# A gated attention block on one core: the up products of two token tiles made together, as seven block products instead of eight

## The chip, the cores and the metric

The kernel runs on one core of a Trainium2 chip. The metric is the time of one execution on the device, in microseconds (us); the lower, the better. A core has TensorE (PE in the profile; its weight loads are PEld), VectorE (DVE), ScalarE (ACT), GpSimd (POOL) and SyncE (SP, which issues most of the DMAs). Each engine works off its own queue in order.

## What is computed

Both branches see the same normalised tokens. One is attention over the last 512 rows of a cache with 32 heads, the other an MLP with a squared relu, which gates the first.

```python
xn = _layernorm(x, axis=-1)                    # x: 2048 tokens x 640
s = _A_ref(xn, A_k_cache, A_v_cache, A_wq, A_wo)   # attention, 32 heads of 128, times wo
h = jnp.einsum("bsd,df->bsf", xn, w1) + b1     # 640 -> 1728
r = jnp.where(h > zero, h, zero)
h = r * r
out = jnp.einsum("bsf,fd->bsd", h, w2) + b2    # 1728 -> 640
return x + s * _silu(out)
```

## The kernel before

Everything lies transposed: features on the 128 partitions, tokens along a row. The 2048 tokens are four tiles of 512 (`NT`). D = 640 is five slices of 128 (`DC`), and F = 1728 is fourteen chunks (`FC`): thirteen of 128, and one of 64 that stands fourth in the order (`rp`, line 66).

TensorE multiplies in a shortened form of float32 (`F32R`). To keep the precision, each operand is split in two: a high part, which ACT makes by a copy into that form, and a low part, the difference, which VectorE or GpSimd makes with two inputs from SBUF. A product is then three matmuls (high by high, high by low, low by high: `triple`, line 560, and `products`, line 97) of 128 x 128 by 128 x 512. The chunk of 64 packs both parts of the weights side by side and needs two.

The work has two stages.

1. **MLP of the first three tiles** (`mlp_step`, line 483, over `steps`, line 464). A step (t, f) makes one chunk of the hidden layer, `up` (line 416): 15 matmuls into a bank `ph`; ACT adds the bias and the relu, GpSimd squares, ACT and VectorE split the square (`square_split`, line 383). It then makes `down` (line 448) of the step before, 15 matmuls into five banks `py` that collect over all chunks. So the split of h has the time of one down and one up. All of w1 and w2 is split during the first tile (`split_w`, line 373) and stays in SBUF. The normalisation of the next tile runs beside (`ln_load`, `ln_block`, `ln_var`, `ln_root`, `ln_rows`, `ln_chunk`, lines 141 to 202), and each tile's split input is stored for attention (`spill`, line 338). After its last chunk a tile's gate is made (`gate`, line 467) and stored.
2. **Attention** (from line 538), 128 units of one head and one tile, laid out by a plan with hand-set times, with parts of the fourth tile's MLP before and behind it.

The order is set in two ways. Instructions given through `Ordered` (line 69: `pe`, `dve`, `act`, `pool`, `sp`) keep the order in which they are written, on their engine. Those given through `nc.tensor`, `nc.vector` and so on may be moved by the scheduler when the program is built, within what their data allow. `pe.addr_align` puts the next instruction of TensorE at a chosen place in a block of 256 instructions, with empty ones ahead of it; attention relies on it (`align`, line 1035), and `LEAD_STEPS` (line 22) spreads empty ones over some steps ahead.

PSUM has eight banks of 128 x 512: two for `ph`, five for `py`, one (`psx`) for odd jobs.

Of the kernel before, what the change touches and what calls it, by code (L numbers as in the profile page):

```python
# [21 lines left out]
LEAD_SLOT, LEAD_PADS, LEAD_STEPS = 76, 5, range(19, 23)  # L22
# [3 lines left out]
def kernel(  # L26
# [24 lines left out]
    LN_AT = {t: (3, 7) if t == LATE else (5, 9) for t in range(1, NTILE)}  # L51
# [45 lines left out]
    def products(ps, pairs, first=True, last=True):  # L97
        n = len(pairs)
        for i, ((ah, al), (bh, bl)) in enumerate(pairs):
            nc.tensor.matmul(ps, ah, bh, start=first and i == 0, stop=False)  # L100
            nc.tensor.matmul(ps, ah, bl, start=False, stop=False)  # L101
            nc.tensor.matmul(ps, al, bh, start=False, stop=last and i == n - 1)  # L102

    psx = ctx.enter_context(tc.tile_pool(name="psx", bufs=1, space=PSUM))

    FO, FA = FC - 3, FC - 4
    keep = ctx.enter_context(tc.tile_pool(name="keep", bufs=1))
    mctx, wctx, hctx = ExitStack(), ExitStack(), ExitStack()
    wpa = wctx.enter_context(tc.tile_pool(name="mwa", bufs=1, side="right"))
    wpb = mctx.enter_context(tc.tile_pool(name="mwb", bufs=1))  # L110
    xp = mctx.enter_context(tc.tile_pool(name="mx", bufs=2))
    hp = mctx.enter_context(tc.tile_pool(name="mh", bufs=2))
    ps_h = hctx.enter_context(tc.tile_pool(name="ps_h", bufs=2, space=PSUM, side="right"))
    ps_y = mctx.enter_context(tc.tile_pool(name="ps_y", bufs=DC, space=PSUM))

    w1s, w2s = [], []
    for f, (f0, n) in enumerate(chunks):
        wp = wpa if f < FO else wpb
        if n < P:
            w1s.append([wp.tile([P, DC, 2 * n], F32R, name=f"w1s{f}")])  # L120
        else:
            if f < FA:
                w1p = [wp.tile([P, DC, n], F32R, name=f"w1s{f}_{i}") for i in range(2)]
            else:
                two = keep.tile([P, 2, D], F32R, tag="ot", name=f"w1s{f}", bufs=4)
                w1p = [two[:, i, :].rearrange("p (c n) -> p c n", n=n) for i in range(2)]
            w1s.append(w1p)
        w2s.append([wp.tile([P, D], F32R, name=f"w2s{f}_{i}") for i in range(2)])
# [4 lines left out]
    pad(wpa, 480)  # L133

    def ln_tile(t, b):
        tag = "stage" if b < 2 else "mr"
        return xp.tile([P, D], F32, tag=tag, name=f"xb{t}_{b}")
# [38 lines left out]
    def ln_rows(t, mv):  # L176
        pm = psx.tile([P, NT], F32, tag="x", name=f"pmv{t}")
        nc.tensor.transpose(pm[: 2 * NB, :P], mv.rearrange("p a b -> p (a b)"), ident)
# [181 lines left out]
    def split_parts(f, k):  # L360
        n = chunks[f][1]
        if k == 0 and n < P:
            return [w1s[f][0][:, :, i * n : (i + 1) * n] for i in range(2)]
# [9 lines left out]
    def split_w(f, k):  # L373
        if f < FC:
            split_hi(f, PRE[f, k], k)
            split_lo(f, PRE[f, k], k, dve)
            if 9 <= f < FC - 1:
                load_part(f + 1, k)
# [864 lines left out]
```

## Time and profile before

| what | value |
|---|---|
| median of three runs | 1958.72 us (1958.66 to 1958.79) |
| span of the profiled execution, first to last instruction | 1956.9 us |
| the profiled execution's own time | not listed apart; the runs' median lies 1.8 us above the span |
| TensorE, matmuls | 8612, busy 1949.2 us |
| VectorE busy | 1537.3 us (79%) |
| ACT busy | 1187.6 us (61%) |
| GpSimd busy | 1376.7 us (70%) |
| the MLP stage of the first three tiles | from about 10 to 298 us |

How to read the lines: a line of the timeline has start, duration, engine, source line, operation, what is written `<-` what is read, shape, count, and in brackets how long the engine was idle before and who ended that. A group has its total busy time and the mean in ns of one. Many operations carry L77, the line of the helper `Ordered`; there the names of the tiles tell which they are. A matmul record is longer (389 ns) than its distance from the next, as they overlap; distances are what counts.

### The profile page before, as it was taken

What the parts mean: (1) busy time and instruction counts of PE and PEld (TensorE: products, weight loads), DVE (VectorE), ACT (ScalarE), POOL (GpSimd) and SP (SyncE); (2) the same over time, 40 slices, a digit from 0 to 9 for tenths busy, and PEclk for the clock granted to TensorE, in tenths of its full rate; (3) what the DMA queues carried; (4) which work ended last, traced back from release to release, by engine and by line L of the source; (5) the groups of instructions that cost most, each with busy time, mean ns of one, the idle gap of its engine ahead of it and who ended that gap; (6) DMA issues with size and microseconds to landing.
All of it is one profiled execution on the core that took longest, in us unless ns stands there. A gap on an engine that the chain in (4) does not pass through costs nothing.

```text
span 1956.9 us, 28182 instructions
## 1 busy us (share of the span) xinstructions
PE 1949.2 (100%) x8612; PEld 1612.5 (82%) x8612; DVE 1537.3 (79%) x2638; ACT 1187.6 (61%) x2040; POOL 1376.7 (70%) x757
## 2 busy tenths in 40 slices
PE   9999999999999999999999999999999999999998
PEld 7888888888888888888888888888888888888887
DVE  6523337788888888888888878888888888888865
ACT  5432336766666666666666676666666666666643
POOL 2121226888888888888888888888888888888841
PEclk9999999999999999999999999999999999999999
DMA  6330454333333332332335434433333333332353
GB/s 189 88 119 28 185 198 130 97 94 92 93 92 93 92 92 92 92 92 93 93 91 179 141 117 109 114 114 114 114 113 114 113 114 114 98 92 92 85 189 118
DMA packets 127892, 219.13 MB, mean 112 GB/s; under 512 B 23452, under 2 KB 38086, under 8 KB 126470
## 3 DMA queue, kind: packets, MB, share of 16 engines
q1 hardware_dynamic: 124742, 202.75, 34.3%
q0 software_dynamic: 2864, 14.42, 1.8%
q8 instruction: 77, 1.26, 0.2%
q14 instruction: 65, 0.53, 0.1%
q10 hardware_dynamic: 144, 0.16, 0.0%
HBM read 193.41 MB, written 23.87 MB: 111 GB/s over the span
## 4 chain that ended last, share of the span: by engine, by line
PE 99%; DVE 0%; DMA 0%; ACT 0%; issue 0%; POOL 0%; POOLq 0%
PE pq L77 22%; PE r L77 22%; PE o L77 18%; PE s L77 18%; PE ph L431 7%; PE ly L77 2%; PE py L101 2%; PE py L100 2%; PE py L102 2%; PE lu L77 2%; PE eu L77 1%; PE ph L398 0%; PE py L454 0%; PE py L453 0%; DMA xb<-in_x_dram 0%; PE px L77 0%
## 5 line engine op out<-in xcount | busy, mean ns | idle before, releaser
L77 POOL TENSOR_TENSOR pt<-e,pt 128x1024 fp32r<-128x1024 f32 x256 | 615.8, 2405 | 113.6 <-ACT pt L77 68.2
L77 PE MATMUL r<-ot,wo 128*128 128x512 f32 x1920 | 496.6, 389 | 0.0
L77 PE MATMUL pq<-ax,wq 128*128 128x512 f32 x1920 | 456.1, 389 | 0.0
L77 PEld LDWEIGHTS pq<-ax,wq 128*128 128x128 f32 x1920 | 360.4, 188 | 75.2 <-DVE q L77 0.4
L77 PEld LDWEIGHTS r<-ot,wo 128*128 128x128 f32 x1920 | 360.5, 188 | 74.8
L77 PE MATMUL o<-pt,wv 128*128 128x512 f32 x1536 | 369.2, 389 | 0.0
L77 PE MATMUL s<-q,wk 128*128 128x512 f32 x1536 | 369.0, 389 | 0.0
L77 DVE TRANSPOSE_TENSOR_REDUCE rdm<-s 128x16 f32<-128x512 f32 x512 | 347.6, 712 | 6.0 <-PE s L77 5.8
L77 ACT ACTIVATE e<-e 128x1024 f32<-128x1024 f32 x256 | 269.8, 1054 | 123.8 <-DVE e L77 80.5
L77 PEld LDWEIGHTS o<-pt,wv 128*128 128x128 f32 x1536 | 288.3, 188 | 60.1 <-POOL pt L77 0.4
L77 PEld LDWEIGHTS s<-q,wk 128*128 128x128 f32 x1536 | 288.4, 188 | 59.8
L77 DVE TENSOR_TENSOR e<-s,bm 128x512 f32<-128x512 f32 x512 | 312.3, 665 | 5.8 <-DMA bm<-m_d 5.4
L77 POOL TENSOR_TENSOR su<-e,e 128x1024 f32<-128x1024 f32 x128 | 309.2, 2415 | 0.0
L77 ACT ACTIVATE pt<-e 128x1024 fp32r<-128x1024 f32 x256 | 271.9, 1062 | 6.9
L77 DVE TENSOR_TENSOR acc<-r,acc 128x512 f32<-128x512 f32 x300 | 203.6, 679 | 12.7 <-PE r L77 12.4
L77 ACT ACTIVATE rdm<-rdm 32x64 f32<-32x64 f32 x384 | 97.7, 254 | 182.1 <-DVE rdm L77 179.0
L77 DVE TRANSPOSE_TENSOR_REDUCE rds<-su 128x32 f32<-128x1024 f32 x128 | 158.4, 1237 | 0.3 <-POOL su L77 0.3
L77 DVE TENSOR_TENSOR ot<-o,ot 128x512 fp32r<-128x512 f32 x128 | 88.5, 692 | 86.1 <-ACT ot L77 86.1
L77 ACT ACTIVATE q<-pq 128x512 fp32r<-128x512 f32 x128 | 76.7, 599 | 113.6 <-PE pq L77 113.6
L431 PE MATMUL ph<-xT,w1s 128*128 128x512 f32 x585 | 139.0, 389 | 0.0
L431 PEld LDWEIGHTS ph<-xT,w1s 128*128 128x128 f32 x585 | 109.7, 188 | 22.8
L77 ACT ACTIVATE rds<-rds 32x32 f32<-32x32 f32 x384 | 89.7, 234 | 60.1 <-DVE rds L77 56.6
(137 smaller groups left out, 1942.3 us busy)
## 6 DMA issues: line engine op xcount, KB each, us to landing
bm<-m_d SPq DMA_DIRECT2D x128, 256.0 KB, 3.2
bs<-s_d SPq DMA_DIRECT2D x128, 256.0 KB, 4.0
qr<-in_wq_dram SPq DMA_DIRECT2D x64, 320.0 KB, 4.5
or<-in_wo_dram SPq DMA_DIRECT2D x64, 320.0 KB, 4.7
kr<-in_kT_dram SPq DMA_DIRECT2D x64, 256.0 KB, 4.3
vr<-in_v_dram SPq DMA_DIRECT2D x64, 256.0 KB, 4.3
xT_d<-xT POOLq DMA_DIRECT2D x6, 1280.0 KB, 7.6
ax<-xT_d SPq DMA_DIRECT2D x4, 1280.0 KB, 11.3
```

The lines of the kernel that those rows point to most:

```text
L77: ins = method(*args, **kwargs)
L100: nc.tensor.matmul(ps, ah, bh, start=first and i == 0, stop=False)
L101: nc.tensor.matmul(ps, ah, bl, start=False, stop=False)
L102: nc.tensor.matmul(ps, al, bh, start=False, stop=last and i == n - 1)
L431: nc.tensor.matmul(ph, w1s[f][i][:, c, :], xs[j][:, c, :], start=k == 0, stop=k == len(order) - 1,)
```

## The change

The up products of the second and third tile (T1, T2) are no longer made chunk by chunk within each tile. Twelve of the full chunks form six pairs. For a pair, the weights are a 2 x 2 matrix of blocks (two chunks by even and odd slices of D; the fifth slice is left over), and the inputs are another (even and odd slices by the two tiles). Strassen's method in Winograd's form makes the four results with seven block products instead of eight, with sums of weight blocks (`w_sums`, GpSimd), of input blocks (`t_sums`, VectorE, once) and of results (in PSUM). `rest` adds the fifth slice in the ordinary way. The chunk of 64 and the last chunk stay ordinary.

As up and down of a tile no longer go together, the squares of both tiles are stored to DRAM (`square_out`), and a third part loads them with w2, splits both again (`c_load`, `c_prep`) and makes all 28 down steps (`c_down`). With it move: the normalisation of T1 and T2, both now within the first tile's steps (`first_step`); that of the fourth tile, over the pairs and the first down steps; the spills; w1 and w2 are no longer kept as a whole but reloaded (the last four chunks of w1 stay for the fourth tile); the memory pools are cut anew. The new MLP functions use `Ordered` throughout, except `t_sums` and `ln_chunk`.

```diff
-LEAD_SLOT, LEAD_PADS, LEAD_STEPS = 76, 5, range(19, 23)
+LEAD_SLOT, MID_SLOT, LEAD_PADS, LEAD_STEPS = 76, 101, 5, range(4, 21)
...
+    def square_out(t, f, r):
+        pool.tensor_tensor(r, r, r, op=ALU.mult)
+        sp.dma_start(h_m[t, f][: chunks[f][1], :], r)
+
+    def r_tile(t, f):
+        return pc.tile([P, NT], F32, tag="r", name=f"r{t}_{f}", bufs=4)
...
+    def up_end(t, f, ph):
+        r = r_tile(t, f)
...
+        act.activation(r, ph, AF.Relu, bias=b1_sb[:, f : f + 1])
+        if t:
+            return square_out(t, f, r)
...
+    def t_sums(q):
+        e, o = 2 * q, 2 * q + 1
+        (h1, l1), b12, b22 = XS[T1], XC.pop((T2, e)), XC.pop((T2, o))
+        t = [tmp(f"ts{q}_{k}") for k in range(4)]
+        eng = nc.vector
+        eng.tensor_tensor(t[0], b12, raw(h1[:, e, :]), op=ALU.subtract)
+        eng.tensor_tensor(t[0], t[0], raw(l1[:, e, :]), op=ALU.subtract)
+        eng.tensor_tensor(t[1], b22, t[0], op=ALU.subtract)
+        eng.tensor_tensor(t[2], b22, b12, op=ALU.subtract)
+        eng.tensor_tensor(t[3], raw(h1[:, o, :]), t[1], op=ALU.subtract)
+        eng.tensor_tensor(t[3], t[3], raw(l1[:, o, :]), op=ALU.add)
+        SUMS["t", q] = t
+
+    def t_split(q):
...
+            act.activation(hi[:, q, :], t, AF.Copy)
+            dve.tensor_tensor(lo[:, q, :], t, raw(hi[:, q, :]), op=ALU.subtract)
...
+    def w_sums(p):
...
+        pool.tensor_tensor(s1, a21, a22, op=ALU.add)
+        pool.tensor_tensor(s2, s1, a11, op=ALU.subtract)
+        pool.tensor_tensor(s3, a11, a21, op=ALU.subtract)
+        pool.tensor_tensor(s4, a12, s2, op=ALU.subtract)
+        SUMS["w", p] = s
...
+    def w_split(p, k):
...
+        for hi, lo, src in pieces:
+            act.activation(hi, src, AF.Copy)
+            dve.tensor_tensor(lo, src, raw(hi), op=ALU.subtract)
...
+    def w_first(p):
+        PB[p] = b = {"a": ps_h.tile([P, NT], F32, tag="ph", name=f"wa{p}")}
+        prod(p, 1, b["a"], True)
+
+    def w_seed(p):
+        b = PB[p]
+        for k in "yx":
+            b[k] = ps_y.tile([P, NT], F32, tag="py", name=f"w{k}{p}")
+        act.activation(b["x"], b["a"], AF.Copy)
+
+    def w_second(p):
+        b = PB[p]
+        prod(p, 5, b["y"], True)
+        b["p5"] = xp.tile([P, NT], F32, tag="p5", name=f"p5_{p}", bufs=2)
+        act.activation(b["p5"], b["y"], AF.Copy)
+        prod(p, 6, b["a"])
+        dve.tensor_tensor(b["y"], b["a"], b["p5"], op=ALU.add)
+        prod(p, 2, b["x"])
+        rest(p, 0, 0, b["x"])
+        up_end(T1, PAIRS[p][0], b["x"])
+
+    def w_third(p, between=None):
+        b = PB.pop(p)
+        prod(p, 7, b["a"])
+        dve.tensor_tensor(b["x"], b["a"], b["p5"], op=ALU.add)
+        if between:
+            between()
+        prod(p, 3, b["y"])
+        rest(p, 0, 1, b["y"])
+        up_end(T2, PAIRS[p][0], b["y"])
+        prod(p, 4, b["a"])
+        rest(p, 1, 0, b["a"])
+        up_end(T1, PAIRS[p][1], b["a"])
+        rest(p, 1, 1, b["x"])
+        up_end(T2, PAIRS[p][1], b["x"])
...
+        if f == 12:
+            t_sums(0)
+            t_split(0)
+            t_sums(1)
...
+    for f in range(FC):
+        first_step(f)
...
+    w_sums(0)
+    for k in range(3):
+        w_split(0, k)
+    up(T1, FC - 1)
+    down(FC - 1, home(FC - 1, 1), HS.pop(FC - 1), PY[0])
+    gate(0, gate_tile, range(2))
+    up(T1, rp)
+    gate(0, gate_tile, (2,))
+    w_first(0)
+    w_seed(0)
+    up(T2, rp)
+    w_load(2)
+    w_sums(1)
+    w_split(1, 0)
+    w_second(0)
+    gate(0, gate_tile, (3, 4))
+    w_split(1, 1)
+    w_split(1, 2)
+    NP = len(PAIRS)
+    for p in range(1, NP):
+        more = p + 1 < NP
+        if p + 2 < NP:
+            w_load(p + 2)
+        w_first(p)
+        w_seed(p)
+        if more:
+            w_sums(p + 1)
+        w_third(p - 1)
+        if more:
+            w_split(p + 1, 0)
...
+        if p in (2, 3):
+            spill(p - 1, XS[p - 1])
+            for b in range(2):
+                ln_block(LATE, 2 * (p - 2) + b)
+        if p == 3:
+            ln_var(LATE)
+            LN[LATE] = ln_root(LATE)
...
+        w_second(p)
+        if more:
+            w_split(p + 1, 1)
+            w_split(p + 1, 2)
...
+    for m in range(2 * FC):
+        t, f = CS[m]
+        if m + 3 < 2 * FC:
+            c_load(m + 3)
+        if m + 2 < 2 * FC:
+            for k in range(2):
+                c_prep(m + 2, k)
...
+        if m == OPEN:
...
+            load_raw("q", 0, 0)
+            load_raw("k", 0, 0)
...
+                load_xT(0, 0, i, slice(0, DC))
...
+        if m in LEAD_STEPS:
+            pe.addr_align(BLOCK, lead_slot(m))
+        c_down(m)
```

In `w_split(p, k)`, k = 0 splits the first chunk's four slices (512 columns), k = 1 the four sums (two pieces of 512), k = 2 the second chunk's odd slices (256) and the two left-over slices (128 each).

507 lines of the change are left out of this document (331 added, 176 removed).

## The prediction, on record before the result

> **What bounds the kernel now.** I read the page first, then the chain of waits, then who waited for whom, then the windows of the stage that changes. All times are microseconds, all matmuls 128x128x512 in three passes.
>
> ```profile
> span 1956.9 us, 28182 instructions
> ...
> PE 1949.2 (100%) x8612; PEld 1612.5 (82%) x8612; DVE 1537.3 (79%) x2638; ACT 1187.6 (61%) x2040; POOL 1376.7 (70%) x757
> ...
> PE 99%; DVE 0%; DMA 0%; ACT 0%; issue 0%; POOL 0%; POOLq 0%
> ```
>
> ```profile
> PE pw L77 <- POOL mv L77: 1.7, 1, 1.7
> PE px L77 <- ACT xb L77: 0.8, 2, 0.5
> ```
>
> ```profile
> 88.19 3.40 PE ph L431 x15
> 94.99 3.40 PE ph L431 x15
> 122.19 2.30 PE ph L398 x10
> 298.23 2.72 PE s L77 x12
> ```
>
> TensorE is the chain: 99% of it, and it waited only 1.7 + 0.8 us, all before the first matmuls. One up block of 15 matmuls takes 3.40, so a matmul is 0.2267, and one step (up and down) is 94.99 - 88.19 = 6.80. TensorE never waits in the MLP. So the change can win only by leaving matmuls out, and loses whatever it makes TensorE wait.
>
> ```profile
> 54.00:108.00 54.00, 54.00 (x241) 44.61 (x240) 27.20 (x36) 22.62 (x35) 8.34 (x8) 1.00 0.25 74
> 108.00:288.00 180.00, 180.00 (x796) 148.26 (x795) 59.71 (x110) 54.28 (x83) 42.24 (x53) 1.00 0.36 134
> 280.00:290.00 10.00, 10.00 (x46) 8.28 (x45) 3.79 (x6) 4.25 (x7) 1.04 (x1) 1.00 1.00 391
> ```
>
> Columns: PE, PEld, DVE, ACT, POOL busy, clock, DMA share, GB/s. In the rest of tile 0 (first row) VectorE is busy half the time; in tiles 1 and 2 (second row) a third. There is room on average. What follows is about order, not averages.
>
> **The matmuls removed.** Twelve full chunks form six pairs. A pair took 2 chunks x 2 tiles x 15 = 60 matmuls. Now it takes 7 products x 2 steps x 3 passes = 42, and the fifth slice of D stays ordinary: 4 x 3 = 12. That is 54. So 6 x 6 = 36 matmuls go: 8612 becomes 8576, and 36 x 0.2267 = **8.16 us** is all there is to win. The spare slots ahead of 17 of the steps cost nothing, since the twelve score matmuls at 298.23 carry such slots between them and still take 12 x 0.2267 = 2.72; the first group of them can be longer, which I bound at 0 to 0.5.
>
> **What each pair's chain costs.** I follow iteration p of the new loop from t = 0, the end of w_second(p-1) on TensorE.
>
> ```profile
> 91.69 0.69 ACT L77 ACTIVATE r<-ph,b_sb 128x512 f32<-128x512 f32 x1 [0.98 <-PE ph L431]
> 92.27 0.73 ACT L77 ACTIVATE w1s<-w1r 128x640 fp32r<-128x640 f32 x1
> 92.45 1.04 POOL L77 TENSOR_TENSOR r<-r 128x512 f32<-128x512 f32 x1 [5.76 <-ACT r L77]
> 94.19 0.69 DVE L77 TENSOR_TENSOR h<-r,h 128x512 fp32r<-128x512 f32 x1
> ```
>
> An up block ended at 88.19 + 3.40 = 91.59; the relu began 0.10 later, the next ACT instruction 0.58 after that, the square 0.86 after the block's end and it ended at 1.90. In the new loop the same relu and square run, and behind the relu on ACT come five high parts of w_split(p, 1) and (p, 2), from 0.68 on. VectorE needs them for five low parts, and only behind those, in program order, stands the sum x = a + p5 of w_third. TensorE is waiting for that sum: prod(4) writes bank a, which the sum reads. TensorE gets there after 6 + 6 + 6 + 3 = 21 matmuls: t = 4.76. On GpSimd, behind the square, stand the four sums w_sums(p+1), ready long before, on 128x256.
>
> ```profile
> 1865.68 2.42 POOL L77 TENSOR_TENSOR pt<-e,pt 128x1024 fp32r<-128x1024 f32 x1 [3.05 <-ACT pt L77]
> 1868.05 2.88 POOL L77 TENSOR_TENSOR su<-e,e 128x1024 f32<-128x1024 f32 x1
> 1866.10 2.54 DVE L77 TENSOR_TENSOR lh<-lr,lh 128x512 fp32r<-128x512 f32 x1 [0.95 <-ACT lh L77]
> 1908.59 1.71 POOL L77 TENSOR_TENSOR l1w<-l1r,l1w 128x640 fp32r<-128x640 f32 x1 [1.43 <-ACT l1w L77]
> 1908.17 0.69 DVE L77 TENSOR_TENSOR acc<-acc,fx 128x512 f32<-128x512 f32 x1
> 1908.78 2.06 DVE L77 TENSOR_TENSOR lh<-lh,lh 128x512 fp32r<-128x512 f32 x1
> L77 DVE TENSOR_TENSOR acc<-r,acc x300: 636/676/692, 395.6 to 1892.3; 128x512 f32<-128x512 f32 x150
> ```
>
> These rows say how the two engines meet. A low part (two SBUF inputs) takes 0.69; at 1866.10 it took 2.54, because GpSimd was inside an instruction; the following GpSimd instruction then took 2.88 where its kind takes 2.41. At 1908.78 the same. They take turns: whoever waits gets the next turn, even where the other has more queued. The last row is the exception that matters too: 300 additions with one input in PSUM never took over 0.692, however busy GpSimd was. The hand-over is a little before the recorded ends: 1908.78 + 2.06 - 0.69 = 1910.15 is 0.15 before GpSimd's 1910.30, and GpSimd's 1868.05 + (2.88 - 2.41) = 1868.52 is 0.12 before VectorE's 1868.64.
>
> ```profile
> L77 POOL TENSOR_TENSOR pt<-e,pt 128x1024 fp32r<-128x1024 f32 x256 | 615.8, 2405 | 113.6 <-ACT pt L77 68.2 <-POOL wv L77 23.4 <-POOL wk L77 13.4
> L77 POOL TENSOR_TENSOR su<-e,e 128x1024 f32<-128x1024 f32 x128 | 309.2, 2415 | 0.0
> L77 POOL TENSOR_TENSOR wk<-kr,wk 128x512 fp32r<-128x512 f32 x62 | 80.8, 1303 | 50.6 <-ACT wk L77 50.6
> L77 POOL TENSOR_TENSOR l1w<-l1r,l1w 128x320 fp32r<-128x320 f32 x1 | 0.9, 876 | 0.0
> L389 DVE TENSOR_TENSOR h<-r,h 128x512 fp32r<-128x512 f32 x26 | 18.0, 692 | 88.0 <-ACT h L388 88.0
> L77 DVE TENSOR_TENSOR acc<-lsg,acc 128x256 f32<-128x256 f32 x2 | 0.8, 422 | 1.1 <-ACT lsg L77 1.1
> L77 DVE TENSOR_TENSOR o<-o,bs 128x512 f32<-128x512 f32 x128 | 86.7, 677 | 0.0
> ```
>
> GpSimd on 256 columns: from 1303 (512) and 876 (320) an estimate of 0.74. VectorE: 0.69 for 512, 0.42 for 256, and by the same slope an estimate of 0.29 for 128; the sum into PSUM 0.68. The first low part gets its turn at 1.90 - 0.15 = 1.75. Each turn of both is then (low part - 0.12) + (0.74 - 0.15): 1.16, 1.16, 0.89, 0.76. So the low parts begin at 1.75, 2.91, 4.07, 4.96, 5.72; the last ends at 6.01 and x is summed by 6.6. TensorE wanted it at 4.76: **a wait of 1.9 in an iteration**. Without GpSimd's sums it would be 1.75 + 0.61 + 0.61 + 0.35 + 0.21 + 0.21 + 0.68 = 4.4, no wait (0.61 is the distance of 1908.78 from 1908.17): the cover is there, but only 0.35 thick.
>
> This happens where w_sums(p+1) exists, p = 1 to 4. At p = 1 the gates of tile 0 stand before the low parts (2.1 by the same count). At p = 4 the sum y = a + p5 is late as well, as the last tile's statistics, its root and a Sqrt table load stand ahead of it on VectorE and ACT:
>
> ```profile
> L77 DVE BATCH_NORM_STATS2 st<-xb 128x6 f32<-128x320 f32 x32 | 13.9, 473 | 5.5 <-DMA xb<-in_x_dram 5.5
> L163 ACT ACT_TABLE_LOAD x2 | 2.6, 1283 | 0.0
> ```
>
> Iteration 3's own wait included, a low part ends near t = 12.1 there; behind it four statistics (4 x 0.47 = 1.9), the table load (1.28) and the root's small instructions, in all an estimate of 3.4 to 5, then y (0.7): 16.2 to 17.8. prod(7) of iteration 4 wants y at 15.5, so it waits 0.7 to 2.3. The low parts behind it come late too, but then GpSimd's sums are half done. For both together I take 2.5, between 1.9 and 3.7. **Sum: 2.1 + 1.9 + 1.9 + 2.5 = 8.4.** Bounds: 0, if the hand-overs cost nothing, and 14, below.
>
> The Trainium skill, page "SBUF — State Buffer", section "Who interferes with whom", states the lock for the whole instruction: the second to issue "fully blocks". By that, with no early hand-over, a turn is 0.69 + 0.74 = 1.43, the sum ends near 7.9, the wait is 3.2, and the four come to about 13. The rows above show the turns but a hand-over 0.12 to 0.15 early, so the measured turn is used.
>
> **The end of tile 0.** The second tile's normalisation and twelve sums t_sums with eight low parts move into tile 0, on VectorE. Let 0 be the start of up(0, 12). Its h is split by 94.19 + 0.69 - 88.19 = 6.7. TensorE reaches down(13) after five blocks, 17.0, and needs h13 split, behind t_sums(1). If all twelve sums come after 6.7: 12 x 0.69 + 4 x 0.61 + w2 0.81 + h 0.69 = 12.2, and GpSimd's square and w_sums(0) take five turns between, some 3.3: 22.2, a wait of 5.2. If the first six run earlier, in VectorE's gaps, 4.1 less: 1.1.
>
> ```profile
> L77 DVE TENSOR_TENSOR w2s<-wr,w2s 128x640 fp32r<-128x640 f32 x6 | 4.9, 810 | 0.0
> ```
>
> ```profile
> 108.01 0.75 DVE L472 SCALAR_TENSOR_TENSOR sg<-py,b_sb,sg 128x512 f32<-128x512 f32 x1 [6.33 <-ACT sg L471]
> 108.68 0.68 DVE L389 TENSOR_TENSOR h<-r,h 128x512 fp32r<-128x512 f32 x1
> ```
>
> Here an instruction not held to program order (the gate's, written later) ran ahead of the split of h written earlier. t_sums is on nc.vector, not held either, so I take **1.5** (0 to 5.2).
>
> **The rest: 0.** A second-product step now loads 320 + 256 KB in 3.40, 169 GB/s; the window at 280 moved 391. VectorE gets 0.81 + 0.69 = 1.5 per step of 3.40 and ACT about as much, prepared two steps (6.8) ahead; if GpSimd's work on the last tile's chunks takes turns there, 6.8 is the cover. The 28 new stores of squares go behind loads on SP, and four r tiles cover them. The large reads for attention are behind loads on SP's queue:
>
> ```profile
> L77 POOL DMA_DIRECT2D xT_d<-xT x16 | 8.9, 556 | 0.0
> ```
>
> ```profile
> ax<-xT_d SPq DMA_DIRECT2D x4, 1280.0 KB, 11.3
> ```
>
> Tiles 1 and 2 are spilled from GpSimd's queue in iterations 2 and 3, 0.56 an issue, behind squares for which TensorE does not wait. SP issues a step's load three steps (10.2) ahead; behind two such reads it could come 1.1 late, twice: 0 to 2.2, taken 0. ACT's copy from bank to bank has no row; the PSUM rows are near 0.6 to 0.7 and it has 6 us. Attention is unchanged.
>
> **Sum:** -8.16 + 8.4 + 1.5 = +1.7 on the span of 1956.9. The runs' median 1958.72 lies 1.8 above the span, which I carry along: **1960.5**; its own range, with waits from 4.2 to 12, is 1954.8 to 1962.6.
>
> **Rivals.** (1) *The low parts are not interrupted*: VectorE keeps its turn, the sum is there at 4.4, and only 0 to 1.5 remains: 1950.6 to 1952.1, and with waits below 4.2 still under 1954.8. For it: at 4.4 there is no wait, and VectorE averages a third. Against it: the rows at 1866 and 1908. (2) *Slower: the backlog at the end of tile 0.* t_sums(0) isn't moved up; h13 comes at 22.2 and TensorE waits 5.2 before down(13). With the pair waits: -8.16 + 8.4 + 5.2 = +5.4, 1964. It decides from the point where all waits pass 12. For it: VectorE's work in the last three steps exceeds TensorE's time. Against it: the reordered gate. The Trainium skill, page "TensorE: Matmul & The Clock Gate", section "Part 1: The HAM clock gate", says an idle window of about 3.4 us halves the clock; by that the wait of 5.2 would cost some 1.7 more, 1966. No run here shows it: the clock column reads 1.00 throughout. (3) *The change doesn't cut the count*: 8612 matmuls remain, and the time is 1958.7 or above.
>
> **Numbers.** Forecast 0.38; (1) 0.32; (2) 0.28; (3) 0.02. About 0.2% (3.9 us) is what can be told from no change. Faster: (1), 0.32. Within: the forecast and half of (3), 0.39. Slower: (2) and the other half, 0.29. The range takes in most of (1) and (2): 1951.5 to 1965.
>
> **What would show it.** PE x8576. Waits of PE for VectorE ahead of prod(4), four times near 1.9; VectorE low parts of 1.2 and more while GpSimd is in w_sums; one wait ahead of down(13). If the low parts stand 0.61 apart, rival 1 holds. If PE waits for a DMA in the second products, the zero of that part was wrong.

## The result, and the profile after

The changed kernel takes 1976.24 us (median of 4 runs, 1975.77 to 1977.58), the kernel before 1958.76 beside it: a ratio of 1.0091, 95% interval 1.0077 to 1.0105. It is slower by 17.5 us, outside the forecast range of 1951.5 to 1965. The profiled execution, the slowest of the four (1977.58), has a span of 1975.8, 18.9 above that of before.

The page of the changed kernel: span, busy times (with the number of instructions), and the chain of waits.

```profile
span 1975.8 us, 28654 instructions
...
PE 1949.8 (99%) x8576; PEld 1605.6 (81%) x8576; DVE 1604.2 (81%) x2717; ACT 1225.4 (62%) x2122; POOL 1426.0 (72%) x798
...
PE 92%; issue 3%; DVE 2%; DMA 1%; ACT 0%; SPq 0%; POOL 0%; ACTq 0%; DVEq 0%; POOLq 0%
```

The 36 matmuls are gone (8576). But TensorE is 92% of the chain where it was 99%. Who it waited for (total, times, longest):

```profile
PE wa L77 <- DVE wx L77: 5.8, 4, 1.8
PE py L77 <- ACT h L77: 3.9, 1, 3.9
PE ph L77 <- DVE w1s L77: 2.3, 2, 1.8
PE py L77 <- DVE h L77: 1.7, 1, 1.7
...
PE py L77 <- ACT cw L77: 1.2, 1, 1.2
PE s L77 <- DVE sgl L77: 0.9, 1, 0.9
...
```

The first row is the wait that the prediction priced, four times. The next three lie in the first tile, where it expected none before down(13). The windows there (PE, PEld, DVE, ACT, POOL busy, clock, DMA share, GB/s); the last is the stretch that the prediction showed of the kernel before:

```profile
54.00:80.00 26.00, 24.16 (x106) 19.38 (x105) 20.04 (x34) 10.04 (x17) 7.98 (x5) 1.00 0.52 161
80.00:90.00 10.00, 4.36 (x13) 2.88 (x12) 9.73 (x11) 4.12 (x7) 4.73 (x5) 0.68 0.50 192
90.00:100.00 10.00, 10.00 (x38) 8.02 (x37) 8.40 (x12) 4.78 (x8) 4.11 (x3) 0.81 0.57 206
...
54.00:108.00 54.00, 46.52 (x189) 36.92 (x188) 42.06 (x62) 22.79 (x39) 17.86 (x13) 0.91 0.53 173
```

From 80 to 90 us TensorE worked 4.36 of 10, and the granted clock, 1.00 throughout before, fell to 0.68 and 0.81. From 54 to 108 VectorE works 42.06 where it worked 27.20.

To see where 18.9 us came from, I take the matmuls of the trace by their starts: the time between two of them less 0.2267 for each one between is lost time. From the first up matmul to the first score, before loses -0.1 in all. The first tile is counted up to the first product of the first pair. The table also has the kernels of the experiments, to which the text below goes back. The three losses are those of one profiled execution, the medians those of all; for h_all the profiled one is the fastest of five (1965.61), for i_halfsums the slowest of nine (1965.78).

| kernel | first tile | pairs | second products, last gate | median us | ratio to before (95%) |
|---|---|---|---|---|---|
| the change | 12.4 | 9.5 | 4.2 | 1976.24 | 1.0091 (1.0077 to 1.0105) |
| e_rows | 11.4 | 10.6 | 3.6 | 1976.57 | 1.0086 (1.0071 to 1.0101) |
| e_sums | 10.9 | 4.9 | 4.5 | 1972.16 | 1.0064 (1.0049 to 1.0079) |
| e_w2dve | 10.9 | 9.2 | 4.1 | 1974.83 | 1.0076 (1.0059 to 1.0093) |
| e_end | 11.2 | 9.5 | 1.9 | 1973.59 | 1.0071 (1.0056 to 1.0086) |
| f_held2 | 13.8 | 12.4 | 4.0 | 1980.95 | 1.0113 (1.0096 to 1.0130) |
| f_held12 | 18.1 | 10.8 | 4.7 | 1985.26 | 1.0135 (1.0120 to 1.0150) |
| f_warm | 11.0 | 10.1 | 16.6 | 1988.73 | 1.0156 (1.0141 to 1.0171) |
| f_three | 18.1 | 4.6 | 1.4 | 1975.89 | 1.0091 (1.0076 to 1.0106) |
| g_behind | 18.3 | 9.7 | 5.8 | 1985.52 | 1.0136 (1.0121 to 1.0152) |
| g_tsums | 16.5 | 15.2 | 4.6 | 1985.59 | 1.0139 (1.0124 to 1.0154) |
| g_early | 17.0 | 14.1 | 3.9 | 1986.17 | 1.0146 (1.0129 to 1.0163) |
| g_all | 17.0 | 6.5 | 1.2 | 1976.46 | 1.0090 (1.0075 to 1.0105) |
| h_pipe | 14.2 | 9.2 | 1.5 | 1977.66 | 1.0097 (1.0083 to 1.0111) |
| h_pearly | 9.8 | 9.2 | 5.0 | 1975.61 | 1.0085 (1.0072 to 1.0099) |
| h_all | 9.0 | 4.6 | 1.3 | 1967.70 | 1.0046 (1.0032 to 1.0060) |
| i_halfsums | 8.2 | 4.6 | 1.6 | 1964.42 | 1.0027 (1.0017 to 1.0037) |
| i_nomult | 6.4 | 4.7 | 1.3 | 1964.04 | 1.0026 (1.0016 to 1.0036) |
| i_subdve | 10.3 | 4.6 | 1.8 | 1967.84 | 1.0044 (1.0029 to 1.0059) |

For the change: 12.4 + 9.5 + 4.2 - 8.16 = 17.9 of the 18.9; 0.3 more lies ahead of the first up matmul, 0.2 between the first score and the last matmul, 0.1 is of before, and 0.4 of the very end. Attention is unchanged, as predicted. (The 32 added transposes of f_warm are not counted as matmuls, and their time stands in its first tile.) The loss of the first tile varies by some 1.5 between kernels that do the same there (10.9 to 12.4); differences below that say nothing. Most of that spread is the clock: the 14 matmuls behind the long wait take 6.17 in the change, and 4.86 and 4.82 in e_sums and e_end, whose order there is the same.

### The profile page after: what moved, and what is told of

Its sections match the earlier page's. It is cut to its first block, busy times and chain, and to the rows that moved or that the text cites. A ratio compares the mean times of both kernels' runs of the same rounds, so it can differ in the third digit from the quotient of the medians.

```text
span 1975.8 us, 28654 instructions
## 1 busy us (share of the span) xinstructions
PE 1949.8 (99%) x8576; PEld 1605.6 (81%) x8576; DVE 1604.2 (81%) x2717; ACT 1225.4 (62%) x2122; POOL 1426.0 (72%) x798
## 4 chain that ended last, share of the span: by engine, by line
PE 92%; issue 3%; DVE 2%; DMA 1%; ACT 0%; SPq 0%; POOL 0%; ACTq 0%; DVEq 0%; POOLq 0%
PE r L77 22%; PE pq L77 22%; PE s L77 18%; PE o L77 18%; PE py L77 4%; PE ly L77 2%; PE ph L77 2%; PE lu L77 2%; PE wa L77 1%; PE wx L77 1%; PE wy L77 1%; PE eu L77 1%; DMA w1r<-in_w_dram 0%; DVE st L77 0%; DMA mv_d<-lr 0%
## 5 line engine op out<-in xcount | busy, mean ns | idle before, releaser
L77 POOL TENSOR_TENSOR wo<-or,wo 128x640 fp32r<-128x640 f32 x64 | 101.0, 1579 | 30.7 <-ACT wo L77 30.7
L77 POOL TENSOR_TENSOR wv<-vr,wv 128x512 fp32r<-128x512 f32 x64 | 83.3, 1302 | 51.8 <-ACT wv L77 51.8
```

The source lines that it names most:

```text
L77: ins = method(*args, **kwargs)
```

## The wait in the pairs

The timeline of iteration p = 2 of the changed kernel (start, duration):

```profile
147.34 2.26 DVE L77 TENSOR_TENSOR ws<-ws,ws 128x512 fp32r<-128x512 f32 x2 [2.62 <-ACT ws L77]
...
149.13 1.06 POOL L77 TENSOR_TENSOR ws<-ws,wp 128x256 f32<-128x256 f32 x1
149.52 0.95 DVE L77 TENSOR_TENSOR wc<-wp,wc 128x256 fp32r<-128x256 f32 x1
...
150.15 0.92 POOL L77 TENSOR_TENSOR ws<-wp,wp 128x256 f32<-128x256 f32 x1
150.40 1.55 DVE L77 TENSOR_TENSOR wl<-wp,wl 128x128 fp32r<-128x128 f32 x2
...
151.88 0.69 DVE L77 TENSOR_TENSOR wx<-wa,p 128x512 f32<-128x512 f32 x1
...
152.62 0.74 PE L77 MATMUL wa<-T,wc 128*128 128x512 f32 x2 [1.76 <-DVE wx L77]
```

Five low parts take from 147.34 to 151.95, each stretched by a GpSimd sum between; the sum x follows and TensorE waits 1.76. Counted by starts the four waits ahead of prod(4) are 0.96, 1.92, 1.92 and 1.68, with 0.78 ahead of prod(7) at p = 4: 7.3, and with 0.1 of restart behind each 7.8. The forecast was 8.4. The theory is turn-taking on VectorE; its rival, that TensorE waits for something else, for instance a bank or the high parts.

**e_sums** puts the weights' sums behind the products that wait:

```diff
-        if more:
-            w_sums(p + 1)
         w_third(p - 1)
         if more:
+            w_sums(p + 1)
             w_split(p + 1, 0)
```

> Edit: in the pair loop GpSimd's w_sums(p+1) stands behind w_third(p-1) instead of ahead of it. Theory A (the engines take turns instruction by instruction where both read two inputs from SBUF): the low parts run without interruption, the four waits ahead of prod(4) (0.96, 1.92, 1.92, 1.68, with restarts 6.9 in all) fall below 1 in all; the wait for y at p = 4 (0.9) stays; about 1970. Rival B: the five high and low parts are late by themselves, through ACT's order; then the four waits stay near 1.9 and the time near 1976.

The same stretch in its timeline:

```profile
145.66 1.71 DVE L77 TENSOR_TENSOR ws<-ws,ws 128x512 fp32r<-128x512 f32 x2 [2.62 <-ACT ws L77]
147.30 0.41 DVE L77 TENSOR_TENSOR wc<-wp,wc 128x256 fp32r<-128x256 f32 x1
147.64 0.48 DVE L77 TENSOR_TENSOR wl<-wp,wl 128x128 fp32r<-128x128 f32 x2
148.04 0.68 DVE L77 TENSOR_TENSOR wx<-wa,p 128x512 f32<-128x512 f32 x1
```

The low parts now follow each other, the last is done at 148.12 and TensorE does not wait; the pairs lose 4.9 instead of 9.5. What stays is 0.96 at p = 1, where the gates of the first tile stand ahead on ACT and VectorE (read from the order, not tested), 0.61 at p = 3, and the sum y at p = 4, now 1.33 late. Turn-taking is shown as the cause of the larger part.

## The second products and the last gate

Here the prediction had 0 to 2.2 and took 0. In the changed kernel the load of the last square, the issue at 294.45, stands on SP's queue behind the second pair of large reads:

```profile
293.03 0.90 SPq L77 DMA_DIRECT2D ax<-xT_d  x2
...
294.45 0.52 SPq L77 DMA_DIRECT2D ch<-h_m  x1
...
306.72 0.63 ACT L77 ACTIVATE ch<-ch 128x512 fp32r<-128x512 f32 x1 [12.89 <-DMA ch<-h_m]
...
314.91 0.69 ACT L77 ACTIVATE sgl<-py,b_sb 128x512 f32<-128x512 f32 x1 [2.73 <-DMA g_d<-sgl]
```

The split of that square starts 12.27 after the issue, and TensorE loses 1.6 around 307. The last row is the fifth tile of the last gate, which waits for a buffer that still has to be stored; TensorE waits for it 1.1 ahead of the first scores. **e_end** moves the second pair of reads one step later and gives the fifth gate tile a buffer of its own:

```diff
                 load_raw(kind, 0, 1)
+        if m == OPEN + 3:
             open_xT(0, 1)
...
-        lambda d: pools["ep"].tile([P, NT], F32, tag=f"wv{d % 2}", name=f"sgl{d}", bufs=G),
+        lambda d: (
+            pools["ep"].tile([P, NT], F32, tag="q0", name=f"sgl{d}", bufs=AHEAD + 1)
+            if d == DC - 1
+            else pools["ep"].tile([P, NT], F32, tag=f"wv{d % 2}", name=f"sgl{d}", bufs=G)
+        ),
```

> Edit, in two places that are read apart: the second pair of xT reads (2 x 1280 KB) is issued one step later, behind the last load of a square; and the last of the five gate tiles of the third tile gets a buffer of its own. Theory A: the wait of 1.8 ahead of the last second-product step comes from its load standing behind those reads, and the wait of 1.2 ahead of the first scores from the fifth gate tile waiting for the first one's store: both go, minus 3.0, about 1973. Rival B: the last loads are late because memory is busy; then the first wait stays near 1.8, or a wait ahead of the second q product appears.

Both waits are gone and this part loses 1.9 (a wait of 0.8 at 216 for a square's low part stays). The two causes are shown together, not each by itself. h_pipe, without this edit, had 1.5 here, and g_behind 5.8. That the queue is near its limit, and that a load comes late or not by when the ones ahead of it went out, would fit, but is not shown.

## The first tile

The chain of the long wait, in the timeline of the changed kernel. Up(9) ends at 74.4:

```profile
78.39 0.69 DVE L213 TENSOR_TENSOR xc<-xc,mr 128x512 f32<-128x512 f32 x1 [2.29 <-DMA mr<-mv_d]
78.46 3.03 POOL L213 TENSOR_TENSOR xc<-xc,mr 128x512 f32<-128x512 f32 x2 [5.25 <-DMA mr<-mv_d]
80.27 2.97 DVE L214 TENSOR_TENSOR xc<-xc,mr 128x512 f32<-128x512 f32 x3 [1.18 <-POOL xc L213]
82.12 0.63 ACT L215 ACTIVATE xT<-xc 128x512 fp32r<-128x512 f32 x1 [6.99 <-DVE xc L214]
82.66 0.67 ACT L77 ACTIVATE r<-ph,b_sb 128x512 f32<-128x512 f32 x1
...
85.45 0.79 PE L77 MATMUL py<-h,w2s 128*128 128x512 f32 x1 [3.93 <-ACT h L77]
...
87.96 6.17 PE L77 MATMUL py<-h,w2s 128*128 128x512 f32 x14 [1.71 <-DVE h L77]
```

Read it upwards. TensorE waits for the high part of h9; that comes late because its relu (82.66) runs 8 us after its product; ACT stood idle 6.99, not for the relu, but for the high part of the third tile's first chunk (82.12), which is ahead of it in the queue: step 9 is written with that chunk ahead of its up. And that chunk waits for the rows of mean and root, which go through DRAM and arrive at 78.4. So ACT's in-order queue carries a wait for a transfer into the path of the MLP. The second wait, 1.71, is for the low part of h9, behind more of the chunks' work on VectorE. Then 14 matmuls take 6.17, 0.43 apiece: the clock is halved.

**e_rows** and **e_w2dve** were a first attempt. The one gives the third tile's chunks one step more; the other makes four low parts of w2, which the change had also given to GpSimd, on VectorE again. (The cuts in this section are parts of the edits.)

```diff
-    CH = {1: {7: (0, 1), 8: (2, 3), 9: (4,)}, 2: {9: (0,), 10: (1, 2), 11: (3, 4)}}
+    CH = {1: {7: (0, 1), 8: (2, 3), 9: (4,)}, 2: {10: (0,), 11: (1, 2), 12: (3, 4)}}
```
```diff
-            split_lo(f, PRE[f, k], k, pool if k and 5 <= f < 9 else dve)
+            split_lo(f, PRE[f, k], k, dve)
```

> Edit: the second tile's chunks are normalised in steps 10 to 12 of tile 0 instead of 9 to 11; nothing else. Theory A: the wait of 6.4 us ahead of down(9) (and the half clock of about 2.6 us behind it) comes from ACT's relu standing in its queue behind the first chunk's high part, which waits for VectorE, which waits for the mean and root rows on their way through DRAM (row store to landing 7.3 us). One step later the rows are there: the wait and the half clock go, minus 9, about 1967. Rival B: VectorE has too much work in tile 0 altogether; then the wait only moves to steps 11 to 13 or to down(13), and the time stays within 2 of 1976.

> Edit: the low parts of w2 for chunks 5 to 8 are made by VectorE instead of GpSimd. Theory A: at step 8 of tile 0 GpSimd's low part of w2 (1.6 to 2.0 us) holds off VectorE's chain of low parts and small instructions, and TensorE waits 2.1 for w1; without it that wait and the 0.8 in step 5 shrink below 0.5 each: minus 2 to 2.5, about 1974. Rival B: VectorE is simply full there; 0.8 more per step makes the waits longer, plus 1 to 3.

e_rows decides nothing: the chunks are not held to the written order, and the scheduler put them where they had been, the first one again ahead of the relu of up(9); the waits are the same. In e_w2dve the wait near 62 fell from 2.0 to 1.35; the two at down(9) come to 4.9 idle, where the change has 5.6 and e_sums, with the same order there, 5.1. All this is within the spread of the first tile.

**The clock.** f_warm adds only 32 transposes ahead of down(9), as long as TensorE would idle:

```diff
+        if f == 10:
+            pw = psx.tile([P, NT], F32, tag="x", name="pz")
+            for _ in range(32):
+                pe.transpose(pw[:, :P], ident, ident)
```

> Nothing is moved; 32 transposes of a constant tile into a spare bank are added ahead of down(9), where TensorE idles 3.9 and then 1.7 us with the change. Theory (the matmuls at 0.427 in place of 0.2267 behind that gap come from the clock, which an idle stretch over about 3.4 us halves): the data come no sooner, so down(9) still ends its wait near 88, but the matmuls behind it take 0.227: 2.5 to 3 us less, about 1973.5, clock 1.00 at 80 to 100. Rival (the matmuls are slow because they wait for operands or for the bank): they stay at 0.43, 1976 or more.

TensorE in its timeline, and the first line of its waits:

```profile
80.82 3.66 PE L77 MATMUL pz<-ident 128*128 128x128 f32 x32
84.59 0.50 PE L77 MATMUL py<-h,w2s 128*128 128x512 f32 x1
87.09 3.46 PE L77 MATMUL py<-h,w2s 128*128 128x512 f32 x14 [2.00 <-DVE h L77]
```

```profile
PE py L77 <- issue: 10.7, 1, 10.7
```

The data come hardly sooner (87.09 for 87.96, where all that goes before is some 0.5 earlier), but the 14 matmuls take 3.46 in place of 6.17: the slow ones were the clock's doing, 2.7 us here and 1.4 in e_sums and e_end. Half of the 2.7 is lost again at once, to a new wait of 1.0 + 0.2 for h10 at 94, and the first tile's 11.0 is no less than in e_sums and e_end (10.9 and 11.2). So the work beside TensorE was itself late. That the whole kernel is slower has another reason: the 32 transposes, each with its weight load, shift all later instructions of TensorE by 64 places, and the 10.7 stand 55 matmuls into the second products, just ahead of the first step that has a set place (m = 4), where empty instructions fill the block. The trace has 192 more of them than that of the change, which is 256 less 64.

**The order.** Theory: ACT's and VectorE's queue order, with chunks ahead of relus, costs the 12 us. Rival: the work on VectorE, with GpSimd taking turns, is too much for these steps. f_held2 and f_held12 are e_rows with the chunks of the third tile, or of both, given through the ordered engines; g_behind writes a step's chunks behind its up; g_tsums holds the sums of the inputs (`t_sums`) as well, the second six behind h13; g_early is that with the chunks back in steps 9 to 11. (In the first cut, f_held2 has `t == T2`.)

```diff
-        (nc.vector if t == T1 or t == T2 and c > 2 else nc.gpsimd).tensor_tensor(xc, xc, bc[0], op=ALU.subtract)
...
+        held = t in (T1, T2)
+        v, a, g = (dve, act, pool) if held else (nc.vector, nc.scalar, nc.gpsimd)
+        (v if t == T1 or t == T2 and c > 2 else g).tensor_tensor(xc, xc, bc[0], op=ALU.subtract)
...
-        for t in (T1, T2):
-            for c in CH[t].get(f, ()):
...
-                ln_chunk(t, c)
         HS[f] = up(0, f)
+        for t in (T1, T2):
+            for c in CH[t].get(f, ()):
...
+                ln_chunk(t, c)
```

> The edit of e_rows again (the third tile's chunks one step later), and this time the chunks' instructions on VectorE, ACT and GpSimd keep the written order, so that the relu of up(9) and the square's high part stand ahead of the first chunk's high part on ACT. Theory (ACT's queue holds the relu behind a part that waits for the round trip of the rows through DRAM): the waits of TensorE at 81 to 88 (3.9 + 1.7) go, and with them the half clock of 10 us (some 3): about 1967, the clock 1.00 at 80 to 100 us. Rival (VectorE simply has more work in steps 5 to 13 than these steps last): the wait moves to a later down or to the end of tile 0, in sum nearly as long, 1973 to 1976.

> As f_held2, and the second tile's chunks keep the written order as well. In the trace with the change VectorE has a low part of w1 late at 62, behind these chunks; with the low parts of w1 written first in each step, the wait of 2.0 there should go too if the order of the queue is its cause: 2 below f_held2, about 1965. If VectorE's amount of work is the cause, the chunks only come later and the time stays that of f_held2 or a wait opens behind it.

> As f_held12 (written order kept for the chunks, third tile one step later), but a step's chunks are written behind its up, so that relu, square and split of h stand ahead of them on ACT, VectorE and GpSimd. Theory (what costs is a relu or an h that queues behind a chunk): the waits between 60 and 105 (3.1 + 1.5 + 0.8 + 1.7 + 1.9 in f_held12) and the half clock go; what remains is the end of the tile, where VectorE's sums of the inputs stand ahead of h13 (3 to 5): about 1968 to 1971 against 1985 of f_held12. Rival (VectorE has too little time in these steps, whatever the order): the waits move behind 105 and the time stays above 1977.

> As g_behind, and the sums of the inputs keep the written order too, the second six of them behind the split of h13. Theory: the wait for h13 goes, 2 to 4 below g_behind, unless the first six sums ahead of h13 in step 12 hold it; rival (too little time): the wait moves to the first pair's products, which need the weights' low parts and the sums, and the time stays that of g_behind.

> As g_tsums, with the third tile's chunks back in steps 9 to 11, so VectorE has them done a step earlier. If VectorE's time in steps 10 to 13 is what is short, this gains 2 to 5 on g_tsums; if only the order counts, nothing, or it loses some 1 to 2 since the first chunk again waits for its rows in step 9.

My theory failed five times. In f_held2 the wait at 81 to 88 is gone indeed, but 1.0, 1.9 and 3.4 open at 96, 105 and 114, with a half clock behind the last. In f_held12 and g_behind the first tile loses 18. In g_tsums the wait for h13 stays (5.7), g_early has none there but 3.1 at the first pair's first product, and both lose more in the pairs (15.2 and 14.1 for the change's 9.5): the time is that of g_behind, as the rival had it. g_behind shows one reason, in the timeline of one step with two chunks:

```profile
69.17 0.67 ACT L77 ACTIVATE r<-ph,b_sb 128x512 f32<-128x512 f32 x1
...
73.20 1.41 DVE L77 TENSOR_TENSOR xc<-xc,mr 128x512 f32<-128x512 f32 x2
...
74.65 0.63 ACT L77 ACTIVATE xT<-xc 128x512 fp32r<-128x512 f32 x1 [2.08 <-DVE xc L77]
75.31 0.69 DVE L77 TENSOR_TENSOR xT<-xc,xT 128x512 fp32r<-128x512 f32 x1 [0.70 <-ACT xT L77]
75.92 1.41 DVE L77 TENSOR_TENSOR xc<-xc,mr 128x512 f32<-128x512 f32 x2
77.36 0.63 ACT L77 ACTIVATE xT<-xc 128x512 fp32r<-128x512 f32 x1 [2.08 <-DVE xc L77]
...
79.15 0.67 ACT L77 ACTIVATE r<-ph,b_sb 128x512 f32<-128x512 f32 x1
```

From one relu to the next 9.98 pass, and a step of TensorE is 6.80. ACT and VectorE wait for each other in turn (2.08, 0.70, 2.08): in written order a chunk is a chain through two in-order queues, and everything behind it stands in that chain. The scheduler's order, which I wanted to mend, was better than these five of mine.

The longest wait of g_behind, 5.2 at 117, is another, and f_held2 (3.4) and h_pipe below (3.0) have it too: down(13) waits for h13, whose low part stands on VectorE behind the second six sums of the inputs, most of them stretched by GpSimd. That is the wait that the prediction looked for, in its place.

**Order or amount?** h_pipe cuts each chunk in two halves, a step apart, so that no engine waits for the other within it; h_pearly also makes the third tile's statistics, rows and both tiles' chunks one step earlier, and the sums of the inputs in steps 11 and 12.

```diff
+        for t in (T1, T2):
+            for c in CH[t].get(f - 1, ()):
+                ln_parts(t, c)
         HS[f] = up(0, f)
+        for t in (T1, T2):
+            for c in CH[t].get(f, ()):
...
+                ln_chunk(t, c)
...
-        for t, at_ in ((T1, 2), (T2, 5)):
+        for t, at_ in ((T1, 2), (T2, 4)):
...
-    CH = {1: {7: (0, 1), 8: (2, 3), 9: (4,)}, 2: {9: (0,), 10: (1, 2), 11: (3, 4)}}
+    CH = {1: {6: (0, 1), 7: (2, 3), 8: (4,)}, 2: {8: (0,), 9: (1, 2), 10: (3, 4)}}
```

(`ln_parts` makes the high and low part, `ln_chunk` the rest.)

> The work of the change, its chunks in the same steps, in the written order, but each chunk in two halves: subtraction and multiplication behind a step's up and h, high and low part at the start of the step after. In g_behind each chunk cost VectorE idle 0.7 and ACT idle 2.1 in turn, and a step with two chunks took 10.0 in place of 6.80. Theory (the hand-overs within a step): a step with two chunks falls back to 6.8 to 7.5, the waits of TensorE from 60 to 110 to below 3, and the time to 1968 to 1973, depending on the end of the tile. Rival (the amount of work, VectorE and GpSimd taking turns): VectorE is busy over 9 of 10 there, the waits stay at 8 or more, 1976 or above.

> As h_pipe, with the third tile's statistics, rows and chunks one step earlier, the second tile's chunks one step earlier, and the sums of the inputs in steps 11 and 12 with their parts a step behind, all in the written order. If both the hand-overs and the lack of room at the end of the tile are removed, the first tile waits 2 to 5 in sum: 1966 to 1969. If the amount of work binds, no better than h_pipe.

h_pipe missed: 1977.66, where hand-overs alone would have given 1973 or less. Against g_behind its first tile gains 4, against the change nothing. The 4 need not be the hand-overs' alone, as h_pipe also has the third tile's chunks a step earlier than g_behind; g_early, which has them there too but holds the sums, lost 17.0. h_pearly's first tile loses 9.8, 4.4 less than h_pipe's; its total gains less, as the late load and the wait of the last gate at the end came back (5.0 for 1.5). Room helps, but the waits stay above the 2 to 5 that I expected.

**Together.** f_three (f_held12), g_all (g_early) and h_all (h_pearly) add the edits of e_sums and e_end.

> Four edits at once: f_held12, the sums of the weights behind w_third (e_sums), the second pair of large reads one step later and the fifth gate tile in a buffer of its own (e_end). By the theory that these are separate causes the gains add: about 10 + 2 (held12) + 5 (sums) + 4 (end) = 21 less than with the change, about 1956 to 1958, level with the kernel before or 1 to 2 faster. If they share one cause (too much work beside TensorE), less than 15 of it comes: 1961 or more.

> g_early with the edits of e_sums (5 less) and e_end (4 less), which lie behind tile 0. By addition: 9 below g_early; if g_early comes to 1966, 1957, level with the kernel before. To be clearly faster than before, tile 0 would have to wait less than 4 in sum.

> h_pearly with the edits of e_sums (5 less) and e_end (4 less). By addition 9 below h_pearly: 1957 to 1960 if h_pearly comes to 1966 to 1969, level with the kernel before (1958.6) within 0.1%; below 1956 only if the first tile waits under 3.

Behind the first tile the gains add as expected in f_three and h_all: 9.5 and 8.3 less in the pairs and the second products; g_all gained 10.2 there. The totals that were expected were missed all the same, as the first tile gave less than hoped. h_all is the best version, 1967.70, a ratio of 1.0046 (1.0032 to 1.0060) to before: 8.5 below the change and still 9.1 above before. Its windows:

```profile
90.00:100.00 10.00, 10.00 (x45) 8.00 (x44) 9.71 (x13) 5.50 (x10) 2.61 (x2) 1.00 0.71 262
100.00:110.00 10.00, 7.94 (x35) 6.28 (x34) 9.90 (x15) 4.95 (x9) 2.76 (x3) 1.00 0.24 67
110.00:120.00 10.00, 9.26 (x40) 6.90 (x40) 9.97 (x15) 6.67 (x13) 4.50 (x4) 1.00 0.19 60
```

VectorE (third) is busy 29.6 of 30 us. If that amount is what TensorE waits for, leaving part of it out must take the waits away. These are h_all with one thing changed: i_halfsums leaves out eight of the twelve sums of the inputs, i_nomult the third tile's multiplications; i_subdve gives GpSimd's three subtractions to VectorE.

```diff
-        t = [tmp(f"ts{q}_{k}") for k in range(4)]
+        t = [tmp(f"ts{q}_{k}") for k in range(2)] * 2
...
-        eng.tensor_tensor(t[0], t[0], raw(l1[:, e, :]), op=ALU.subtract)
         eng.tensor_tensor(t[1], b22, t[0], op=ALU.subtract)
-        eng.tensor_tensor(t[2], b22, b12, op=ALU.subtract)
...
```
```diff
+            if t == T1:
-            dve.tensor_tensor(xc, xc, bc[1], op=ALU.mult)
+                dve.tensor_tensor(xc, xc, bc[1], op=ALU.mult)
```
```diff
-            (dve if t == T1 or c > 2 else pool).tensor_tensor(xc, xc, bc[0], op=ALU.subtract)
+            dve.tensor_tensor(xc, xc, bc[0], op=ALU.subtract)
```

> h_all with eight of the twelve sums of the inputs left out (their results are replaced by the two that remain, so the products of the pairs are not the reference's): 8 x 0.69 = 5.5 less for VectorE in steps 11 and 12, where it is busy without a gap. If the amount of its work is what TensorE waits for there, the waits at 100 to 103 and at 113 (2.2 + 0.9 in h_all) go: about 3 less, 1964 to 1965. If another order or a transfer holds them, they stay.

> h_all with the five multiplications of the third tile's normalisation left out (its inputs are only centred): 5 x 0.69 = 3.4 less for VectorE in steps 8 to 10. Amount: the waits at 76 to 87 (2.1 + 0.45 + 0.7) fall by about 1.5 to 3, and those at 100 to 113 too if VectorE carries its backlog along. If the rows' and the chunks' transfers or GpSimd's subtraction hold the 2.1 at 77, it stays.

> h_all with the three subtractions of the third tile that GpSimd makes given to VectorE (0.69 in place of 1.29, and no hand-over from GpSimd to VectorE). If turn-taking and hand-overs bind in steps 8 and 9, 1 to 2 less; if VectorE's amount binds, 0 to 2 more.

The same windows of i_halfsums:

```profile
90.00:100.00 10.00, 10.00 (x46) 8.29 (x45) 9.59 (x13) 5.69 (x10) 2.55 (x3) 1.00 0.89 302
100.00:110.00 10.00, 10.00 (x46) 8.28 (x45) 8.36 (x13) 6.05 (x11) 3.48 (x4) 1.00 0.34 92
110.00:120.00 10.00, 10.00 (x45) 7.88 (x44) 8.72 (x13) 7.42 (x14) 5.22 (x6) 1.00 0.15 57
```

TensorE is busy throughout from 90 to 120: the waits of 2.2 at 101 and 0.9 at 113 are gone. But TensorE came to these steps 2.7 us later than in h_all (up(13) at 103.1 for 100.4), as the wait at 76 was longer this time (3.6 for 2.1) and the clock halved behind it, and that gave VectorE time as well. The fair comparison is i_subdve, where the same happened at 76 and TensorE is as late: with all twelve sums it waits 1.1 at 103 and 0.9 at 114, and VectorE is busy 9.90 and 9.97 of 10 from 100 to 120, where i_halfsums has 8.36 and 8.72 and no wait. So for the last steps of the tile the amount of VectorE's work ahead of the parts that TensorE needs is shown to be the cause, for 2.0 us. The medians agree with what was expected: 1964.42 for h_all's 1967.70 and i_subdve's 1967.84. (In the table the first tile falls only from 9.0 to 8.2, for the reason just given.) i_subdve itself changes nothing that can be told.

In i_nomult the waits at 76 to 87 fell from 3.3 to 0.7, with new ones of 0.5 + 0.5 at 88, and the 2.2 at 101 to 1.3, which less work for VectorE would explain. At 76 this is not the amount of work. VectorE, in h_all:

```profile
76.52 0.69 DVE L77 TENSOR_TENSOR xc<-xc,mr 128x512 f32<-128x512 f32 x1 [1.94 <-POOL xc L77]
...
77.87 0.82 DVE L77 TENSOR_TENSOR w1s<-w1r,w1s 128x640 fp32r<-128x640 f32 x1
```

in i_halfsums:

```profile
77.98 0.69 DVE L77 TENSOR_TENSOR xc<-xc,mr 128x512 f32<-128x512 f32 x1 [3.27 <-DMA mr<-mv_d]
```

and in i_nomult:

```profile
75.16 0.82 DVE L77 TENSOR_TENSOR w2s<-w2r,w2s 128x640 fp32r<-128x640 f32 x1
75.89 1.92 DVE L77 TENSOR_TENSOR w1s<-w1r,w1s 128x640 fp32r<-128x640 f32 x1
```

TensorE waits for the low part of w1. In h_all VectorE is idle 1.94 ahead of it, at the multiplication of the third tile's first chunk: that waits for GpSimd's subtraction, which itself had waited for the first row to arrive from DRAM. In i_halfsums the same multiplication waits 3.27 for the second row, and in i_subdve VectorE is idle 1.21 and 1.30 for the rows. i_nomult has no such multiplication, and the low part comes without idle time; it takes 1.92 for 0.82 beside a subtraction on GpSimd, and 0.7 of the wait stays. So the wait at 76 is again an instruction that waits for the rows, at the head of an in-order queue, now VectorE's. It was 2.1 in h_all, 3.6 in i_halfsums and 3.4 in i_subdve, depending on when the rows came.

**Not settled** is how much of the change's own 12.4 is that round trip, how much hand-overs, and how much amount, since each edit that took one away let another come to the fore.

## Why the prediction was wrong, point by point

- **The matmuls removed**: right, 36, x8576. At the spare slots no loss is seen.
- **Each pair's chain**: right in mechanism and place, and in size: 7.8 for 8.4. p = 2 and 3 took 1.92 each for 1.9. p = 1 took 0.96 for 2.1: the gates ahead of the low parts ended sooner. p = 4 had both waits, 0.78 + 1.68 = 2.5, as taken. The turn from the rows gave the right size: 1.92 for 1.9 at p = 2 and 3. The Trainium skill ("SBUF — State Buffer", section "Who interferes with whom") has the second engine blocked for the whole instruction; the prediction's estimate by that page, about 13 for the four, does not agree with the 7.8 measured.
- In the pairs 1.7 more is lost without a wait in the list: most of the 42 products of six matmuls take 1.40 in place of 1.36. I have no cause for it.
- **The end of tile 0, 1.5 at down(13)**: this step failed. In the changed kernel the first tile loses 12.4, most of it at down(9). The prediction says that the normalisation of T2 (the third tile here, the second there) moves into tile 0, on VectorE, and then counts only the sums of the inputs and the last steps: it priced nothing for that normalisation, nor for the second tile's, which the change squeezes into steps 7 to 9. What it left out are the rows' round trip through DRAM, the chunk's high part on ACT's queue ahead of the relu, and VectorE's load from step 7 on. It had named both that VectorE's work "in the last three steps exceeds TensorE's time" and that instructions not held to program order move; it took the second as a help only.
- At down(13) itself the changed kernel does not wait, but that is no proof of the reasoning. The scheduler moved the first six sums far ahead (83.8 to 100.8); the second six still stand ahead of h13, whose low part ends at 117.72, 0.2 before TensorE gets there. TensorE had by then lost its 12.4. In f_held2, h_pipe and g_behind the wait is there: 3.4, 3.0 and 5.2.
- **The rest, 0**: failed for the second products, 4.2, beyond the bound of 2.2. That the load behind the two large reads comes late was named and taken as 0; it was 1.6. The last gate's buffers (1.1) and the split at 216 (0.8) were not named; the cause of the 0.8 was not followed.
- **Rivals**: the second, a backlog on VectorE in the first tile, was right in kind for part of the loss; in the changed kernel its place was four steps too late and its price, 5.2, less than half of the 12.4. The sentence on the clock that went with it (the Trainium skill, "TensorE: Matmul & The Clock Gate", section "Part 1: The HAM clock gate": an idle window of about 3.4 us halves the clock) is borne out: behind an idle stretch of 3.9 us and a second of 1.7 the matmuls come every 0.427, and 14 of them take 2.7 longer in the change and 1.4 in e_sums and e_end; the prediction's estimate by that page was 1.7.

## What to carry to other kernels

A saving of 0.4% in the bounding engine must be paid for by every in-order queue beside it: add up, step by step, what each engine gets to do in the time that the bounding engine now takes, above all in the stretch into which other work is moved, and mark each instruction that waits for a transfer and what stands behind it on its queue. Averages over a stage (here VectorE half idle) don't show it, and here a better written order alone did not make room; only less work or an earlier start did. Before a hand-written order replaces the scheduler's, count the hand-overs: two in-order engines that took turns on one chain made a step 10.0 long in which VectorE had 6.9 us of work and ACT 3.7 (the window 70 to 80 of g_behind).

## What the runs showed of the hardware

- The same idle stretch can halve the clock or not. Ahead of w1's low part near 62 TensorE idled 1.83 in the changed kernel and 1.84 in f_held2; behind it the clock stayed at 1.00 in the first, and in the second eight matmuls came every 0.43, so 1.6 us were lost. The window behind that stretch, in the changed kernel and in f_held2 (the clock is the last but two):

```profile
64.00:68.00 4.00, 3.59 (x16) 2.91 (x17) 4.00 (x5) 1.52 (x3) 1.96 (x1) 1.00 0.19 63
```

```profile
64.00:68.00 4.00, 3.62 (x9) 2.85 (x10) 4.00 (x5) 1.49 (x3) 1.94 (x1) 0.57 0.23 63
```
 The Trainium skill, in the section named above ("Part 1: The HAM clock gate" of "TensorE: Matmul & The Clock Gate"), calls the window of 3.4 us free-running, which fits; but its idle window of about 3.4 is more than the 1.84 that was enough here, and the measurement decides. The runs of one of these kernels spread by 0.3 to 5.0 us, those of before by 0.1 to 2.3; that the clock is one cause of it is only argued.
- After the waits of 0.15 to 2.0 us in the changed kernel at full clock the second matmul came 0.11 late as well.
- Empty instructions for alignment are not free when many fall in one place: in f_warm TensorE stands still for 10.7 us, with 187 of them between 222 and 240 us (28 there in the changed kernel), and behind that the clock reads 0.50 from 236 to 240.
